# Fourier transform and two expert layers on one core: the first two rounds in written order, outputs of expert 1 kept in DRAM, weights of expert 2 made earlier, column sums by fp32r matmuls

## The chip, the cores and the metric

The kernel runs on one core of a Trainium2 chip. The metric is the time of one execution on the device in microseconds, less is better. The kernel before was timed three times.

## The reference

```python
X = np.fft.fft(np.fft.fft(x, axis=1), axis=2).real     # x: 2 x 3008 x 256
h = X.reshape(6016, 256) @ w_in                          # 256 x 2048
g = h * (1 / (1 + exp(-h)))                              # expert 1
x1 = g @ w_out                                           # 2048 x 256
h2 = x1 @ w_in2                                          # 256 x 2048, expert 2
g2 = max(h2, 0) + alpha * min(h2, 0)
out = g2 @ w_out2                                        # 2048 x 256
```

The weights of both experts come as float64 and are turned to float32 on the chip.

## The kernel before, in words

A float32 product is made of three fp32r products: each operand is split into a high part and a low part (the low part is the operand minus its high part), and high·high, high·low and low·high are summed. So nearly every tile has a `hi` made by ACT and a `lo` made by DVE or POOL.

**Start.** `stage_a` folds the input and makes the first Fourier stage, stores it in DRAM as `ys`, `load_y` (L302) reads it back transposed, `stage_b` (L311) makes the second stage: tiles `z`, six chunks of 502 columns, three for each of the two batches. `first_row` (L345) makes a row term `n` of a chunk by ones-matmuls. `prep_w1` (L389) turns a quarter of `w_in` to float32 (`to_f32`, four DVE steps), splits it, multiplies it by a small Fourier matrix on PE (`cw`, L424), takes a column sum `r` by fp32 matmuls (L428), and splits the result into `wi`. `prep_o1` does the like for `w_out`. The start is under `manual_schedule`: there every engine's queue holds its instructions in the order of the text.

**Rounds.** 96 rounds, one for each chunk and each 128 of the 2048 columns (`ORDER`). Round i: `eo_mm` (L554) makes `pe` and `po` (three matmuls each, L563 to L565); `mm2(i-2)` (L596) adds 12 matmuls of round i-2 into four accumulators `a` (L613 to L617, those of L615 read the low parts `gl`); `silu_split` (L568) makes `t`, `hp`, `t` on DVE (L571, L574, L575), four SiLU on ACT (L578, L579), and calls `low1(i-1)` (L585), which makes the two low parts `gl` of the round before (L591). The low part for s=1 is always on POOL; that for s=0 is on POOL where `lo_pool` says so (rounds up to 29 and 51 to 86), else on DVE. All other work is dealt out over the rounds by `PLAN` (L26): `put(a, b, steps)` (L862) spreads the steps of a key evenly over rounds a to b. In the rounds a planner sets the order on each engine from modelled times, and `leash` (L871) lets a round's dealt-out steps follow only after `t` of the round before and `gl` of the one before that. `i1` to `i3`, `o1` to `o3` are the quarters of expert 1's weights, `x`, `a`, `y`, `c` the second batch's transform, `w2` the conversion of expert 2's weights. A result of a chunk stays in SBUF as `O1[c]`, one of 12 large buffers (`big`) for each chunk.

**Expert 2.** Its first product uses Strassen's seven products on halves. `prep_ws` (L503) makes the sums and splits of the weights (`ws`, sums L523, lows L518), one set (`ws0`) and another (`ws1`); `prep_wo2` (L533) makes the split of the second weights (`wo`, ACT L542 and L165, lows on POOL L166); `split_o1` (L637) makes four differences (`xt`, L651) and five splits (`os`, L660 and POOL L661) of a half chunk. After the rounds, again in written order, 96 steps n follow: `outer(n)` (L684, products 1 and 5 into `ac`, copied by ACT to `e`, L691), `inner(n)` (L693, products 2, 6, 3), `seventh(n)` (L712), the prelu on ACT and DVE, and `mm4(n-2)` (12 matmuls, L773). Steps 0 and 1 hold the two last `mm2`. A plan key of 96 or more is a step: 97 is n = 1.

Of the kernel before, what the change touches and what calls it, by code (L numbers as in the profile page):

```python
# [32 lines left out]
}  # L33
W2_AHEAD = 2
# [4 lines left out]
    ["xs", "xs", "cs", "ch", "e128", "e128"] + [f"wi{g}_{j}" for g in (2, 3) for j in range(4)],  # L39
# [29 lines left out]
def _tables():  # L69
# [35 lines left out]
    c[:, OC0] = m % 2  # L105
# [15 lines left out]
def fft_moe_kernel(  # L121
# [267 lines left out]
    def prep_w1(g):  # L389
# [3 lines left out]
        def steps(h, v):  # L393
# [160 lines left out]
    def eo_mm(i):  # L554
# [3 lines left out]
        z = ZS[divmod(c, NCB)]  # L558
        pe, po = mm_ps(f"pe{i}", CW), mm_ps(f"po{i}", CW)
        for ps, j in ((pe, 0), (po, 2)):  # L560
            at = 128 * j + 128 * q
            hi, lo = (WI[1, g, 2 * h + k][:, at : at + 128] for k in range(2))
            nc.tensor.matmul(ps, hi, z[:, j, :], start=True, stop=False)  # L563
            nc.tensor.matmul(ps, lo, z[:, j, :], start=False, stop=False)  # L564
            LAST["pe", i] = nc.tensor.matmul(ps, hi, z[:, j + 1, :], start=False, stop=True)  # L565
        return pe, po

    def silu_split(i, pe, po):  # L568
# [221 lines left out]
    if True:  # L790
        with tc.manual_schedule():
# [23 lines left out]
            for h in range(2):  # L815
                load_y(0, h, 0)
# [86 lines left out]
        for pg in range(2):  # L903
            steps = prep_ws(pg)
            put(*PLAN[f"ws{pg}"], steps[:8])
            put(*PLAN[f"ws{pg}b"], steps[8:])
# [109 lines left out]
```

## Time and profile before

| | us |
|---|---|
| median of 3 runs | 974.41 |
| lowest, highest | 973.65, 975.18 |
| profiled execution | 972.72 |
| its span, first to last instruction | 970.9 |

| engine | busy us | share of the span |
|---|---|---|
| PE (matmuls) | 954.2 | 98% |
| DVE | 782.9 | 81% |
| ACT | 709.8 | 73% |
| POOL | 413.4 | 43% |

Busy time is the union of an engine's instructions. The mean granted TensorE clock over the span is 0.995 of full speed.

### The profile page before, as it was taken

The page shows a single profiled execution, that of the slowest core. Times are in us where ns is not written, and L with a number is a line of the kernel's source. Part 1 is how long each engine was busy: PE and PEld are TensorE (multiplying, and loading weights), DVE is VectorE, ACT ScalarE, POOL GpSimd, SP SyncE. Part 2 cuts the span into 40 slices and gives each one's busy share as a digit, 9 for nine tenths or more (in the row PEclk, how much of TensorE's full clock was granted, in tenths as well). Part 3 has the DMA queues.
Part 4 walks back from the last instruction along what each step waited for, and adds up shares of the span by engine and source line. Part 5 has one row for each costly group of instructions (what it writes and reads, how often), then busy time and mean ns, then how long its engine had stood idle before and what let it go on. Part 6 is the DMA issues. An engine that isn't in the chain of part 4 may idle for free.

```text
span 970.9 us, 14465 instructions
## 1 busy us (share of the span) xinstructions
PE 954.2 (98%) x5234; PEld 824.8 (85%) x5234; DVE 782.9 (81%) x1324; ACT 709.8 (73%) x1413; POOL 413.4 (43%) x356
## 2 busy tenths in 40 slices
PE   8999999999999999999999999999999999999997
PEld 6788887788888888887789999999999999999996
DVE  6778999787787888996688787887888888787875
ACT  3567667575576766777888887887878888887885
POOL 2468868763266767789522131221312212131200
PEclk9999999999999999999999999999999999999999
DMA  8921000006110120000000000000000000000000
GB/s 275 311 89 44 1 1 22 22 13 190 43 44 17 44 88 6 39 0 1 1 1 24 19 3 23 1 23 1 22 22 1 23 1 22 22 1 23 1 22 22
DMA packets 16039, 37.05 MB, mean 38 GB/s; under 512 B 1632, under 2 KB 11104, under 8 KB 13920
## 3 DMA queue, kind: packets, MB, share of 16 engines
q1 hardware_dynamic: 15968, 36.13, 11.2%
q8 instruction: 41, 0.67, 0.3%
q14 instruction: 30, 0.25, 0.1%
HBM read 26.81 MB, written 9.31 MB: 37 GB/s over the span
## 4 chain that ended last, share of the span: by engine, by line
PE 90%; DVE 4%; ACT 2%; POOL 2%; issue 1%; DMA 1%; SPq 0%; DVEq 0%
PE a L773 27%; PE ac L675 20%; PE a L615 8%; PE a L617 8%; PE a L613 8%; PE b L675 3%; PE pe L563 2%; PE pe L565 2%; PE pe L564 2%; PE po L563 2%; PE po L565 2%; PE po L564 2%; PE psb L321 1%; PE psa L277 1%; POOL gl L591 1%
## 5 line engine op out<-in xcount | busy, mean ns | idle before, releaser
L773 PE MATMUL a<-gh,wo 128*128 128x502 f32 x768 | 268.5, 391 | 0.0
L773 PEld LDWEIGHTS a<-gh,wo 128*128 128x128 f32 x768 | 145.1, 189 | 23.4
L742 DVE SCALAR_TENSOR_TENSOR h<-h,fc,q 128x502 f32<-128x502 f32 x192 | 129.9, 677 | 37.9 <-ACT q L737 35.1
L591 POOL TENSOR_TENSOR gl<-t,gh 128x502 fp32r<-128x502 f32 x96 | 132.7, 1383 | 52.5 <-ACT t L579 30.5
L615 PE MATMUL a<-gl,wo 128*128 128x502 f32 x384 | 147.5, 394 | 2.5 <-POOL gl L591 2.5
L773 PE MATMUL a<-gl,wo 128*128 128x502 f32 x384 | 149.6, 390 | 0.0
L617 PE MATMUL a<-gh,wo 128*128 128x502 f32 x384 | 146.3, 391 | 0.0
L578 ACT ACTIVATE gh<-hp 128x502 fp32r<-128x502 f32 x96 | 59.9, 624 | 114.9 <-DVE hp L574 114.1
L753 DVE TENSOR_TENSOR gl<-h,gh 128x502 fp32r<-128x502 f32 x192 | 140.7, 733 | 0.1
L748 ACT ACTIVATE gh<-h 128x502 fp32r<-128x502 f32 x192 | 118.4, 617 | 2.1 <-DVE h L742 2.1
L613 PE MATMUL a<-gh,wo 128*128 128x502 f32 x384 | 118.7, 395 | 0.5 <-DVE cvi L197 0.5
L737 ACT ACTIVATE q<-h,fc 128x502 f32<-128x502 f32 x192 | 116.9, 609 | 2.8 <-DVE h L720 1.5
L591 POOL TENSOR_TENSOR gl<-hp,gh 128x502 fp32r<-128x502 f32 x65 | 91.5, 1408 | 62.0 <-ACT hp L579 59.9
L651 POOL TENSOR_TENSOR xt<-o 128x252 f32<-128x252 f32 x24 | 16.7, 714 | 187.0 <-ACT q L737 168.3
L571 DVE SCALAR_TENSOR_TENSOR t<-n,sm,pe 128x502 f32<-128x502 f32 x96 | 70.2, 732 | 26.8 <-PE pe L565 22.9
L615 PEld LDWEIGHTS a<-gl,wo 128*128 128x128 f32 x384 | 72.7, 189 | 18.2 <-POOL gl L591 3.7
L613 PEld LDWEIGHTS a<-gh,wo 128*128 128x128 f32 x384 | 72.2, 191 | 16.4 <-ACT gh L578 1.5
L617 PEld LDWEIGHTS a<-gh,wo 128*128 128x128 f32 x384 | 72.7, 189 | 14.5
L773 PEld LDWEIGHTS a<-gl,wo 128*128 128x128 f32 x384 | 72.5, 189 | 7.6
L709 ACT ACTIVATE u<-ac 128x252 f32<-128x252 f32 x96 | 36.6, 381 | 54.6 <-PE ac L675 50.5
L574 DVE TENSOR_TENSOR hp<-t,po 128x502 f32<-128x502 f32 x96 | 64.5, 672 | 12.1 <-PE po L565 7.5
L661 POOL TENSOR_TENSOR os<-o,os 128x252 fp32r<-128x252 f32 x36 | 32.2, 907 | 92.8 <-ACT os L660 92.8
(177 smaller groups left out, 2292.7 us busy)
## 6 DMA issues: line engine op xcount, KB each, us to landing
out_t<-ot SPq DMA_DIRECT2D x24, 251.0 KB, 2.6
x<-in_xs SPq DMA_DIRECT2D x8, 512.0 KB, 5.2
raw_w<-in_wi SPq DMA_DIRECT2D x4, 1024.0 KB, 5.5
raw_w<-in_wo SPq DMA_DIRECT2D x4, 1024.0 KB, 4.8
raw_i<-in_wi SPq DMA_DIRECT2D x3, 1024.0 KB, 8.0
raw_o<-in_wo SPq DMA_DIRECT2D x3, 1024.0 KB, 5.7
y<-ys SPq DMA_DIRECT2D x16, 144.0 KB, 4.1
x<-in_xs SPq DMA_DIRECT2D x2, 1024.0 KB, 4.8
```

The costliest lines, as they stand in the source:

```text
L571: nc.vector.scalar_tensor_tensor(t, E128[c], odd_sb[:, f : f + 1], pe, op0=ALU.mult, op1=ALU.add)
L574: nc.vector.tensor_tensor(hp, t, po, op=ALU.add)
L591: LAST["gl", i] = (nc.gpsimd if s or lo_pool(i + 1) else nc.vector).tensor_tensor(lo, h, hi.bitcast(F32), op=ALU.subtract)
L613: nc.tensor.matmul(ACC1[lb, s], hi, G[i, s][0], start=st, stop=False)
L615: nc.tensor.matmul(ACC1[lb, s], hi, G[i, s][1], start=False, stop=False)
L617: nc.tensor.matmul(ACC1[lb, s], lo, G[i, s][0], start=False, stop=sp)
L675: nc.tensor.matmul(to, w, x, start=start and q == 0, stop=q == 2, skip_group_check=True)
L737: nc.scalar.activation(h["q", i][:, to], source(n, part), AF.Abs, scale=coef(n, i, 1))
L742: nc.vector.scalar_tensor_tensor(h[f"h{i}"][:, to], source(n, part), coef(n, i, 0), h["q", i][:, to], op0=ALU.mult, op1=ALU.add)
L748: nc.scalar.activation(hi, H[n][f"h{i}"], AF.Copy)
L753: nc.vector.tensor_tensor(lo, H[n][f"h{i}"], G[n, i][0].bitcast(F32), op=ALU.subtract)
L773: nc.tensor.matmul(ACC2[lb], w[lb][j], x, start=st and first, stop=sp and last)
```

## The change

`PLAN` is moved and gets new keys; the rest of the diff, cut to its core:

```diff
-    "o0": (0, 2), "c1": (1, 4), "c2": (4, 7), "i1": (5, 10), "o1": (9, 13),
-    "li2": (10, 11), "i2": (14, 20), "lo2": (13, 14), "o2": (19, 24), "li3": (18, 19), "i3": (23, 27), "lo3": (22, 23), "o3": (26, 29),
+    "o0": (2, 3), "c1": (1, 4), "c2": (4, 7), "i1": (4, 9), "o1": (8, 12),
+    "li2": (9, 10), "i2": (12, 18), "lo2": (12, 13), "o2": (17, 22), "li3": (16, 17), "i3": (21, 25), "lo3": (20, 21), "o3": (24, 28),
...
-    "y2": (65, 66), "c5": (67, 77), "w2": (50, 88),
-    "co": (60, 61), "ws0": (62, 80), "ws0b": (84, 92), "ws1": (80, 92), "ws1b": (93, 99),
-    "wo0": (86, 87), "wo1": (90, 91), "wo2": (97, 98), "wo3": (98, 100),
+    "y2": (65, 66), "c5": (67, 77), "w2": (50, 82),
+    "co": (60, 61), "ws0": (62, 80), "ws0b": (84, 92), "ws1": (82, 92), "o1r": (80, 81), "os": (85, 93),
+    "wo0": (87, 90), "wo1": (91, 94), "wo2": (98, 100), "wo3": (100, 102),
+O1_AHEAD = 14
-    ["xs", "xs", "cs", "ch", "e128", "e128"] + [f"wi{g}_{j}" for g in (2, 3) for j in range(4)],
+    ["xs", "xs", "cs", "ch", "e128", "e128"] + [f"big{j}" for j in range(8)],
...
-                r = mm_ps(f"r{g}_{h}", 2)
+                r = mm_ps(f"r{g}_{h}", 4)
                 for q in range(2):
-                    w = t[0][:, 128 * q : 128 * q + 128]
-                    nc.tensor.matmul(r[:, q : q + 1], w, cs[:, OC0 : OC0 + 1], start=True, stop=True)
+                    for j in range(2):
+                        w = e[j][:, 128 * q : 128 * q + 128]
+                        nc.tensor.matmul(r[:, 2 * q : 2 * q + 2], w, co, start=j == 0, stop=j == 1)
...
-                nc.scalar.activation(w, w, AF.Copy, scale=fc[:, 2, f : f + 1])
-            hi, lo = (WO[2, g, j].rearrange("p f e -> p (f e)")[:, h * 512 : h * 512 + 512] for j in range(2))
-            split(hi, lo, v, nc.gpsimd)
+                v = V2["o", g // 2][:, o + 256 * q : o + 256 * q + 256]
+                hi, lo = (WO[2, g, j][:, 2 * h + q, :] for j in range(2))
+                sign = fc[:, 2, f : f + 1]
+                nc.scalar.activation(hi, v, AF.Copy, scale=sign)
+                nc.vector.scalar_tensor_tensor(lo, v, sign, hi.bitcast(F32), op0=ALU.mult, op1=ALU.subtract)
...
-        return i < LO_POOL or 52 <= i < 88
+        return 2 < i < LO_POOL or 52 <= i < 88
-            LAST["gl", i] = (nc.gpsimd if s or lo_pool(i + 1) else nc.vector).tensor_tensor(
+            LAST["gl", i] = (nc.gpsimd if (s and i < NC * NF - 2) or lo_pool(i + 1) else nc.vector).tensor_tensor(
...
+            if f == NF - 1:
+                store_o1(c)
+    def store_o1(c):
+        OD[c] = dp.tile([128, 4 * CW], F32, name=f"od{c}")
+        nc.sync.dma_start(OD[c], O1[c].rearrange("p k n -> p (k n)"))
+    def load_o1r(c):
+        O1[c] = big([128, 4, CW], F32, f"o1r_{c}")
+        nc.sync.dma_start(O1[c].rearrange("p k n -> p (k n)"), OD[c])
...
-            for h in range(2):
-                load_y(0, h, 0)
+            load_y(0, 0, 0)
...
             nc.scalar.activation(ch, cc, AF.Copy)
+            nc.gpsimd.tensor_copy(co, cs[:, OC0 : OC0 + 2])
+            load_y(0, 1, 0, nc.scalar)
...
-            run(s0[:3])
+            run(s0)
             warm(cs[:, FA0 : FA0 + 128], cs[:, :256], WARM[1])
             b00, b01 = stage_b(0, 0), stage_b(0, 1)
             run(b00[:2])
+            run(p0)
             run(b01[:2])
-            run(post1[4:5])
-            first_row(0, 0)
-            run(post1[5:])
-            run(s0[3:])
-            run(p0)
+            ps0 = eo_mm(0, lambda: first_row(0, 0))
+            ps1 = eo_mm(1)
             run(s1[:EARLY_O0])
+            silu_split(0, *ps0, lambda: run(post1[4:]))
+            silu_split(1, *ps1)
...
-        put(n1 - 5, n1 - 1, split_o1(0))
-        for i in range(n1):
+        put(*PLAN["o1r"], [lambda: load_o1r(0)])
+        put(*PLAN["os"], split_o1(0))
+        for i in range(2, n1 - 1):
...
         with tc.manual_schedule():
-            low1(n1 - 1)
+            pe, po = eo_mm(n1 - 1)
+            outer(0)
+            mm2(n1 - 1 - LAG)
+            silu_split(n1 - 1, pe, po)
+            run(plan.pop(n1 - 1, []))
             for n in range(NP + 2):
...
+                c = (n + O1_AHEAD) // 16
+                if (n + O1_AHEAD) % 16 == 0 and c < NC:
+                    load_o1r(c)
...
-                if new:
+                if 0 < n < NP:
                     outer(n)
...
+                if n == 0:
+                    low1(n1 - 1)
```

Each chunk's result goes to DRAM when it is finished and is read back 14 steps before its block of 16 steps (chunk 0's in round 80). The buffers that this frees take the second half of `ws1`, so `ws1` no longer waits for `wi` of the last rounds. The function of `eo_mm` is split in two halves so that something can be called between them, and `silu_split` gets the same; between `hp`, `t` and the SiLU of round 0 stand now the Fourier product, the column sum and the split of the first quarter's second half (`post1[4:]`).

## Rows read from the trace of the kernel before

**Rows 1.** Windows: us, busy of PE, PEld, DVE, ACT, POOL (instructions), granted clock, DMA share, GB/s.

```profile
20.00:40.00 20.00, 17.74 (x98) 15.13 (x99) 15.81 (x29) 9.66 (x24) 4.38 (x3) 0.91 0.98 296
...
140.00:160.00 20.00, 18.92 (x92) 15.26 (x91) 18.14 (x24) 12.50 (x24) 15.12 (x13) 1.00 0.00 1
160.00:180.00 20.00, 18.66 (x81) 14.30 (x79) 14.97 (x19) 12.20 (x22) 19.30 (x15) 1.00 0.08 26
...
400.00:420.00 20.00, 20.00 (x89) 16.53 (x88) 18.28 (x26) 15.20 (x29) 16.34 (x13) 1.00 0.00 1
420.00:440.00 20.00, 20.00 (x89) 16.38 (x88) 17.48 (x21) 15.24 (x29) 16.84 (x13) 1.00 0.01 1
440.00:460.00 20.00, 17.91 (x79) 14.38 (x78) 14.91 (x20) 15.47 (x29) 20.00 (x18) 0.98 0.00 0
460.00:480.00 20.00, 17.85 (x101) 15.32 (x101) 11.24 (x22) 15.89 (x35) 8.15 (x8) 0.94 0.01 1
```

**Rows 2.** Timeline of PE after round 95: start, us, instruction [idle before <-releaser].

```profile
459.12 0.78 PE L615 MATMUL a<-gl,wo 128*128 128x502 f32 x1 [1.69 <-POOL gl L591]
...
468.78 0.50 PE L675 MATMUL ac<-os,ws_6h 128*128 128x252 f32 x2 [1.64 <-ACT e L691]
...
471.37 0.50 PE L675 MATMUL ac<-os,ws_7h 128*128 128x252 f32 x2 [0.27 <-DVE h L710]
```

**Rows 3.** Timeline of POOL in the same stretch.

```profile
454.47 2.95 POOL L661 TENSOR_TENSOR os<-xt,os 128x504 fp32r<-128x504 f32 x2
457.38 2.90 POOL L591 TENSOR_TENSOR gl<-t,gh 128x502 fp32r<-128x502 f32 x2
...
461.47 1.27 POOL L518 TENSOR_TENSOR ws_6l<-v2w,ws_6h 128x512 fp32r<-128x512 f32 x1
```

**Rows 4.** Groups of POOL and DVE: busy us, mean ns of one | idle before.

```profile
L591 POOL TENSOR_TENSOR gl<-t,gh 128x502 fp32r<-128x502 f32 x96 | 132.7, 1383 | 52.5 <-ACT t L579 30.5 <-DVE gl L591 7.6 <-PE pe L565 6.8
L661 POOL TENSOR_TENSOR os<-xt,os 128x504 fp32r<-128x504 f32 x24 | 38.2, 1610 | 50.0 <-ACT os L660 50.0
L661 POOL TENSOR_TENSOR os<-o,os 128x252 fp32r<-128x252 f32 x36 | 32.2, 907 | 92.8 <-ACT os L660 92.8
L651 POOL TENSOR_TENSOR xt<-o,xt 128x252 f32<-128x252 f32 x24 | 22.6, 941 | 0.9
L166 POOL TENSOR_TENSOR wo<-v2o,wo 128x512 fp32r<-128x512 f32 x8 | 11.1, 1400 | 13.7 <-ACT wo L165 13.7
L518 POOL TENSOR_TENSOR ws_5l<-v2w,ws_5h 128x512 fp32r<-128x512 f32 x2 | 3.0, 1520 | 0.0
...
L591 DVE TENSOR_TENSOR gl<-hp,gh 128x502 fp32r<-128x502 f32 x31 | 30.0, 967 | 5.0 <-ACT hp L579 4.6
```

**Rows 5.** Timeline of POOL in round 86 and of PE that uses its results.

```profile
419.08 1.74 POOL L518 TENSOR_TENSOR ws_7l<-v2w,ws_7h 128x512 fp32r<-128x512 f32 x1
420.79 3.44 POOL L166 TENSOR_TENSOR wo<-v2o,wo 128x512 fp32r<-128x512 f32 x2
424.19 1.27 POOL L591 TENSOR_TENSOR gl<-hp,gh 128x502 fp32r<-128x502 f32 x1
...
426.07 0.39 PE L615 MATMUL a<-gl,wo 128*128 128x502 f32 x1
```

**Rows 6.** Timeline of the start: SP's and ACT's queues, and PE in rounds 0 and 1.

```profile
19.56 1.71 SPq L308 DMA_DIRECT2D y<-ys  x4
...
19.93 0.63 ACT L407 ACTIVATE wi<-we 128x512 fp32r<-128x512 f32 x1 [2.33 <-DVE we L404]
...
33.51 0.91 PE L321 MATMUL psb<-cs,y 96*128 96x94 f32 x6 [0.30 <-DVE t L571]
35.41 1.17 PE L321 MATMUL psb<-cs,y 96*128 96x94 f32 x6 [0.99 <-DVE t L575]
...
35.19 0.61 ACT L578 ACTIVATE gh<-hp 128x502 fp32r<-128x502 f32 x1
```

**Rows 7.** The column sums' matmuls: count, duration ns min/median/max.

```profile
L428 PE MATMUL r<-cs,we x32: 165/250/250, 22.3 to 155.3; 128*128 128x1 f32 x32
```

More of the change, by code (lines that the diff above doesn't have):

```diff
@@ L104, in _tables @@
     c[0, SG0 : SG0 + 128] = 1
-    c[:, OC0] = m % 2
+    c[:, OC0 : OC0 + 2] = (m % 2)[:, None]
     c[0, OD0 : OD0 + 128] = m % 2
@@ L228, in fft_moe_kernel @@
     cl = wp.tile([128, SG0 - CD0], F32R, name="cl")
+    co = wp.tile([128, 2], F32R, name="co")
     X = {}
@@ L300, in stage_a, with load_y @@
         return fold, mm, rest
-    def load_y(b, h, kh):
+    def load_y(b, h, kh, queue=None):
         w = (K_PARTS[kh + 1] - K_PARTS[kh]) // 2
@@ L307, in load_y @@
         for j in range(2):
-            last = nc.sync.dma_start(Y[b, kh][48 * j : 48 * j + 48, h, :w, :], src[j])
+            last = (queue or nc.sync).dma_start(Y[b, kh][48 * j : 48 * j + 48, h, :w, :], src[j])
         return last
@@ L424, in fold @@
                         nc.tensor.matmul(to, w, x, start=j == 0, stop=j == len(run_) - 1)
-                r = mm_ps(f"r{g}_{h}", 2)
+                r = mm_ps(f"r{g}_{h}", 4)
                 for q in range(2):
-                    w = t[0][:, 128 * q : 128 * q + 128]
-                    nc.tensor.matmul(r[:, q : q + 1], w, cs[:, OC0 : OC0 + 1], start=True, stop=True)
+                    for j in range(2):
+                        w = e[j][:, 128 * q : 128 * q + 128]
+                        nc.tensor.matmul(r[:, 2 * q : 2 * q + 2], w, co, start=j == 0, stop=j == 1)
                 f = 4 * g + 2 * h
-                nc.scalar.activation(odd_sb[:, f : f + 2], r, AF.Copy)
+                nc.scalar.activation(odd_sb[:, f : f + 2], r[:, ::2], AF.Copy)
             def fold_high():
@@ L490, in coefficients @@
         eng.tensor_tensor(two, two, fc[:, 2, :], op=ALU.mult)
+    QUARTERS = {}
     def slab(home, name):
+        if home[:3] == "big":
+            j, q = divmod(int(home[3:]), 4)
+            if j not in QUARTERS:
+                QUARTERS[j] = big([128, 4, 512], F32R, f"wsb_{j}")
+            return QUARTERS[j][:, q, :]
         if home in ("cs", "ch"):
@@ L552, in fft_moe_kernel, with eo_half @@
     MORE = [False]
-    def eo_mm(i):
+    def eo_half(i, ps, j):
         c, f = ORDER[i]
@@ L558, in eo_mm, with silu_split @@
         z = ZS[divmod(c, NCB)]
-        pe, po = mm_ps(f"pe{i}", CW), mm_ps(f"po{i}", CW)
[L560 to L565, printed above, removed]
+        at = 128 * j + 128 * q
+        hi, lo = (WI[1, g, 2 * h + k][:, at : at + 128] for k in range(2))
+        nc.tensor.matmul(ps, hi, z[:, j, :], start=True, stop=False)
+        nc.tensor.matmul(ps, lo, z[:, j, :], start=False, stop=False)
+        LAST["pe", i] = nc.tensor.matmul(ps, hi, z[:, j + 1, :], start=False, stop=True)
+    def eo_mm(i, between=None):
+        pe, po = mm_ps(f"pe{i}", CW), mm_ps(f"po{i}", CW)
+        eo_half(i, pe, 0)
+        if between:
+            between()
+        eo_half(i, po, 2)
         return pe, po
-    def silu_split(i, pe, po):
+    def silu_split(i, pe, po, between=None):
         c, f = ORDER[i]
@@ L575, in silu_split @@
         LAST["t", i] = nc.vector.tensor_tensor(t, t, po, op=ALU.subtract)
+        if between:
+            between()
         for s, h in ((0, hp), (1, t)):
@@ L628, in mm2 @@
             del G[i, 0], G[i, 1]
+            if f == NF - 1:
+                store_o1(c)
+    OD = {}
+    def store_o1(c):
[4 more added lines that the diff above has]
+        nc.sync.dma_start(O1[c].rearrange("p k n -> p (k n)"), OD[c])
     OS = {}
@@ L902, in fft_moe_kernel @@
         put(*PLAN["co"], [coefficients])
[L903 to L906, printed above, removed]
+        steps = prep_ws(0)
+        put(*PLAN["ws0"], steps[:8])
+        put(*PLAN["ws0b"], steps[8:])
+        put(*PLAN["ws1"], prep_ws(1))
         for g in range(4):
             put(*PLAN[f"wo{g}"], prep_wo2(g))
-        put(n1 - 5, n1 - 1, split_o1(0))
-        for i in range(n1):
+        put(*PLAN["o1r"], [lambda: load_o1r(0)])
+        put(*PLAN["os"], split_o1(0))
+        for i in range(2, n1 - 1):
             pe, po = eo_mm(i)
-            if i >= LAG:
-                mm2(i - LAG)
+            mm2(i - LAG)
             silu_split(i, pe, po)
-            leash(i, plan.pop(i, []))
+            leash(i, plan.pop(0, []) + plan.pop(1, []) + plan.pop(i, []))
         with tc.manual_schedule():
-            low1(n1 - 1)
+            pe, po = eo_mm(n1 - 1)
[3 more added lines that the diff above has]
+            run(plan.pop(n1 - 1, []))
             for n in range(NP + 2):
```

2 lines of the change are left out of this document (removed).

## The prediction

> **What bounds the kernel now.** I read the page first: PE is busy for 954.2 of 970.9 us, no other engine above 81%, and the chain that ended last is PE for 90% of the span. So time can only come from PE's gaps, from its clock, or from matmuls that go away; the change takes none away. The windows in stretches of 20 us then tell where the gaps are [rows 1]. The reader is to see that PE is busy for all 20.00 us of most stretches, while DVE stands at 91% and ACT at 76% beside it, and that four stretches differ: 20 to 40 (start, 2.26 us idle), 140 to 160 and 160 to 180 (1.08 and 1.34), and 440 to 480 (2.09 + 2.15 = 4.24), which is the passage from the rounds to the steps of expert 2. The clock falls in the first and in the last: a mean grant of 0.91 over 20 us is 2 x 0.09 x 20 = 3.6 us at 1.2 instead of 2.4 GHz, which costs 1.8; 0.98 and 0.94 are 0.8 + 2.4 = 3.2 us at the lower level, which cost 1.6. Start 4.1, middle 2.4, passage 5.8: some 12 us are all that there is to gain.
>
> Next the timeline of PE in the passage says who was late [rows 2]: POOL's `gl` (1.69 us), ACT's `e` (1.64), DVE's `h11`/`h12` (0.27); smaller pieces are left. The timeline of POOL says why [rows 3]: `gl` of rounds 94 and 95 queues behind two large `os` lows, and POOL still makes `ws` lows at 461. A round takes 18 matmuls; 89 in 20 us [rows 1] are 0.225 us each, 4.05 us a round.
>
> All sums are against the profiled execution, 972.72 us (span 970.9 and 1.8 around it); the median of the runs is 1.69 higher.
>
> **The passage: -3.7.** Both lows of rounds 94 and 95 go to DVE, `os` and `ws1` are dealt out to round 93, so the waits for POOL and the clock that falls behind them should go. `wo2` moves from step 1, where ACT made both its parts ahead of `e`, to steps 2 and 3, `wo3` to 4 and 5. What is late next: `seventh(0)` needs `h12` on DVE, and before `h11` and `h12` DVE now has four lows of 0.97 [rows 4], between them `hp` and `t` of round 95 and the wait for four SiLU of 0.61 [rows 6]. That is 3.9 + 2 x 0.97 at most for `hp` and `t` + about one SiLU, 6.4, and then `h11` and `h12`. PE has until then mm2(93), mm2(94) (24 x 0.225 = 5.4) and 15 matmuls of half the width (1.7): 7.1 us. They come out about even; I take 0.7, between 0 and the 1.64 of the wait for `e`. In steps 2 to 5 each part of `wo` costs ACT two short copies and DVE two short lows, at the time when ACT also makes `os` of the next half chunk: 0.35 a step, 1.4, an estimate near the 0.27 row; bounds 0 and twice 1.64. Left 2.1 of 5.8: -3.7, from -5.8 to -0.9.
>
> **POOL in rounds 84 to 92: +2.0.** This is the price of making it early. By the plan POOL has there 13 `gl` (13 x 1.383 = 18.0), five lows and three sums of `ws1` and three lows of `ws0` (11, all taken at 1.52: 16.7); four differences `xt` (3.8) and five `os` (3 x 0.907 + 2 x 1.61 = 5.9) [rows 4]. Together 44.4 us in 9 x 4.05 = 36.4: 8 over. The same count for before (13 `gl`, 5 of `ws`, four `wo` of 1.40, four `xt`, one `os`) gives 36, yet the windows show 16.34 and 16.84 of 20 busy, 83%, or 30.2 [rows 1], since the planner runs dealt-out work later than its rounds. By the measured share the new load is 30.2 + 8.4 = 38.6, 2.2 over. There is no cover: in round 86 two `wo` and a `ws` low delayed `gl` until its matmul began 0.6 us after it [rows 5]. Rounds 93 to 95 have room (3 x 2.7 us). I take 2.0, between 0 and 8.0. The conversion `w2`, on DVE and ACT, ends six rounds earlier and so is denser by a fifth in rounds 50 to 82; the stretch 400 to 420 had conversions, `gl` and `ws` with DVE at 91% and no gap on PE [rows 1], so 0; if DVE falls behind, it is in the range of rival C. `wo` on DVE adds eight pairs of short lows in rounds 87 to 94 where the conversions have ended: 0.
>
> **Start: -0.4.** SP issues four `y` loads in 1.71 us [rows 6], 0.43 each. Two of them move to ACT's queue, behind `ch` and ahead of `wi` high (L407). SP could issue at 19.56 only when the stores of `ys` had landed; ACT waits for the stores of the other half too, then issues for 0.85 us, so `wi` high starts at about 20.4 instead of 19.93 and DVE's low and PE's first `cw` go 0.5 later. Against that: rounds 0 and 1 no longer stand behind the second half of the quarter's product on DVE, `t` and `hp` come earlier, and PE's waits for `t` (0.30 and 0.99 [rows 6]) shrink; but the SiLU of round 0, at 35.19 before, now stand behind that product's copy on ACT and so gain little. `gl` of rounds 0 and 1 for s=0 go to a free DVE. Of 4.1 I let 0.9 go and pay 0.5. Bounds -3 and +2 (the ACT queue's wait in full, no gap closed). The DMA engines gain nothing of it that I count. The page "DMA: Bandwidth & Descriptors" of the Trainium skill (section "Issuing engines are not separate DMA queues") says that issuing from a second engine saves only issue time; by it the second half could land 0.85 us earlier, and the sum would be the same, as PE's warming matmuls stand ahead of the reader.
>
> **Middle: -0.9.** `i2`, `o2`, `i3`, `o3` run over rounds 12 to 28 instead of 14 to 29, two rounds ahead of their use, with less overlap. Of 2.4 us idle in 140 to 180 I let the first 0.9 go; the folds of the second batch, which cause most of the rest, keep their rounds. The planner writes a new order, so the bounds are -2.4 and +2.4.
>
> **At nothing.** Column sums: 32 matmul records of one column at 0.25 us before [rows 7], 32 matmuls of two columns after; 0, with a quarter of 8.0 us on either side as bound. Stores and loads of `O1`: 12 transfers on SP with DMA at most 0.16 busy after 140 us in the windows shown [rows 1], reloads asked for 14 steps ahead; 0. In SP's queue a store waits for its accumulators' copies, and behind it wait loads that are dealt out two rounds (8 us) ahead; above 0 only if that is used up. An 0.85 us bound each for six stores is 5.
>
> **Sum.** -3.7 + 2.0 - 0.4 - 0.9 = -3.0: 969.7 for the profiled execution, 971.4 for the median.
>
> **Rivals.**
> A, nothing is paid back: the planner spreads POOL's work into rounds 93 to 95. For it: these rounds have 8 us of room. Against it: the queue of round 86 [rows 5]. Passage -5.3, start -1.0, middle -1.6: -7.9, 966.5.
>
> B, gaps move instead of going: the ACT queue's wait is paid in full and rounds 0 and 1 only trade waits (+1.5), the middle's gaps change place (0). For it: DVE is the bound at the start (15.81 of 20 while PE waits), and its work stays. Passage -3.7, POOL +2.0: -0.2, 974.2.
>
> C, slower: POOL bounds rounds 84 to 92, because the leash puts dealt-out steps ahead of the next `gl`, as in round 86 [rows 5]. All 8.0 us over are paid by PE; `os` comes late, so the clock falls again (1.6 of the passage's gain). -3.7 + 1.6 + 8.0 - 1.3 = +4.6: 979.0. It turns the sign when POOL is over by more than 3.7 + 0.4 + 0.9 = 5.0 us. For it: 8 over by the plan, and the lows now on DVE may hold POOL up: `gl` on DVE takes 0.97 in the rounds [rows 4]. Against it: measured 83%. The Trainium skill, "SBUF — State Buffer", section "SBUF: two separate sides", states that DVE with two SBUF inputs and POOL exclude each other for a whole instruction; by that rule the 16 lows of `wo` moved to DVE and the five of `gl` there still take POOL's time, which makes this rival likelier than its own row says; no row here shows a lock as such.
>
> **How the numbers follow.** Forecast 0.50 (own range 968.5 to 974.0), A 0.17, B 0.18, C 0.15. A measurement of this kernel can tell 0.2%, 1.9 us, from no change: faster is below 972.5, slower above 976.4. Of the forecast 0.70 is faster, 0.28 the same; all of A is faster; B 0.20, 0.60, 0.20; C is slower but for 0.04. Faster 0.35 + 0.17 + 0.04 = 0.56, same 0.14 + 0.11 = 0.25, slower 0.19. The range of 8 in 10 cuts the outer part of A and of C: 965.5 to 978.5.
>
> **What would show it.** Passage: the windows after the rounds with some 2 us idle and the grant at 1.00, no wait of PE for POOL there, one for DVE's `h12` in step 0. Rounds 84 to 92: waits of PE for `gl` on POOL, 2 us in all; 0 is A, 6 or more is C. Start: `wi` high later than 20, its window's idle and grant little changed. Middle: idle between 1 and 2 us. The forecast is wrong if the passage still loses 4 us or more, if rounds 84 to 92 lose more than 5, or if the start moves by more than 3.

## The result, and the profile after

The changed kernel takes 983.19 us in the median of 4 runs (981.85 to 985.64), the kernel before 974.79 beside it (4 runs, 973.65 to 976.09): ratio 1.0089, 95% interval 1.0065 to 1.0112. It is slower by 8.4 us, where 971.4 was forecast. The profiled execution of after took 983.16 us, its span is 981.4, 10.5 longer than that of before.

The windows of after answer to those of before [rows 1]; the columns are the same.

```profile
20.00:40.00 20.00, 16.76 (x87) 13.62 (x87) 13.88 (x28) 8.71 (x20) 1.28 (x1) 0.91 0.92 288
120.00:140.00 20.00, 19.27 (x85) 15.63 (x83) 19.00 (x26) 12.38 (x22) 15.82 (x12) 1.00 0.00 1
140.00:160.00 20.00, 15.77 (x66) 12.35 (x67) 17.84 (x23) 9.58 (x18) 14.62 (x12) 0.91 0.00 0
160.00:180.00 20.00, 20.00 (x94) 16.74 (x94) 16.52 (x23) 13.63 (x25) 15.88 (x12) 1.00 0.09 27
400.00:420.00 20.00, 19.20 (x84) 15.28 (x83) 16.28 (x23) 14.12 (x25) 15.43 (x13) 1.00 0.13 52
420.00:440.00 20.00, 19.20 (x84) 15.37 (x83) 16.75 (x23) 15.15 (x29) 19.50 (x18) 1.00 0.01 1
440.00:460.00 20.00, 19.04 (x82) 14.91 (x81) 19.51 (x24) 14.55 (x29) 19.86 (x15) 1.00 0.00 1
460.00:480.00 20.00, 20.00 (x112) 17.45 (x111) 15.15 (x28) 15.73 (x31) 2.54 (x2) 1.00 0.04 16
480.00:500.00 20.00, 17.93 (x109) 14.87 (x108) 16.91 (x33) 14.20 (x34) 5.67 (x7) 1.00 0.24 88
```

The reader is to see three things. The passage now runs without a gap: 460 to 480 has PE busy for 20.00 us at a clock of 1.00, where before had 17.85 at 0.94. In the middle PE is idle for 4.2 us of one window, at a clock of 0.91. And the passage is now framed by loss: 0.8 to 1.0 us in each window from 400 to 460, with POOL at 19.5 and 19.9 of 20, and 2.07 us in 480 to 500.

A window that starts at a fixed time holds other work in each kernel. So I put marks on the work: the start of the first matmul of `mm2(r)` that reads `gl`, for round r, and of the first of `mm4(s)` that reads `gl`, for step s. The difference of a stage's length between a kernel and the profiled run of before, in us (`mm2(r)` runs in round r+2 and `mm4(s)` in step s+2, so the stages are named by the work, not by the round in which it runs):

```
           to r4  r4-22 r22-32 r32-68 r68-84 r84-93 r93-s0  s0-s5 s5-end  whole
after       +1.2   +2.5   +3.7   -0.1   +2.6   +3.5   -7.3   +4.4   -0.1  +10.4
a_early      0.0   -0.5   +0.6   +0.2   +4.9   +1.9   -7.3   +4.4   -0.6   +3.8
a_start     +0.9    0.0   +2.5   +0.1   +3.4   +3.4   -7.3   +4.4   +0.5   +7.9
a_wo        +1.9   +2.5   +3.8   -0.1   +3.6   +3.9   -7.3   +1.8   +0.2  +10.4
a_w2        +1.3   +2.5   +3.7   -0.1   -0.1   +5.9   -7.3   +4.4   -0.2  +10.0
b_early     +1.3   -1.5   +2.1   -0.1    0.0   +0.2   -1.7   -0.1   -0.5   -0.3
b_pass      +0.8    0.0    0.0    0.0    0.0   +5.0   -7.3   +1.9   -0.7   -0.3
a_nowo      +0.3   -0.5   +0.6   +0.2   +3.3   +1.8   -7.3   -1.1   -0.6   -3.3
b_w95       +2.2    0.0    0.0    0.0    0.0   +6.4   -3.3    0.0   -1.1   +4.2
a_nosums    +2.2   +2.8   +1.8   +0.4   +3.3   +3.6   -7.3   +4.4   -0.9  +10.3
a_late3     +4.6   +2.4   -1.4   +0.5   +3.2   +3.6   -7.3   +4.4   -0.5   +9.7
b_best1     +2.7    0.0    0.0    0.0   +0.5   +3.2   -6.9   +0.6   -0.8   -0.6
b_best1r    +1.2    0.0    0.0    0.0   +0.6   +3.2   -6.9   +0.6   -0.7   -1.9
b_best3     +1.5    0.0    0.0    0.0   +1.0   +1.6   -5.8   +0.6   -0.6   -1.6
```

Read the first line: the passage gave 7.3 us, rounds 68 to 93 took 6.1 and steps 0 to 5 another 4.4, so that the three together lose 3.2. Rounds 4 to 32 lost 6.2 more. The first column is scatter: the kernels that have before's start lie between 0.0 and +2.7 there (8 traces, mean 1.3), those with the written start between 0.0 and +4.6 (7 traces, mean 1.6). The times scatter too: the kernel before took 971.53 to 977.20 us in 19 runs of one session, with a mean granted clock of 0.998 in the fastest and 0.993 in the slowest. So below stages are compared, and a single time proves little.

Two things have to be taken off before a column is read as a loss. The first is work that a new order puts on the other side of a mark. These are PE's matmuls of `pe` and `po` between marks 4 and 22, first in before, then in after:

```profile
59.90:141.50 81.60, 30.71 (x113) 1.00 0.11 38
61.10:145.10 84.00, 28.85 (x104) 1.00 0.10 34
```

After has nine fewer there and nine more behind mark 22; at 0.225 us each that is 2.0 us. So after loses 4.5 in rounds 4 to 22 and 1.7 in 22 to 32, and the same 2.0 changes columns in every kernel with group 3's keys early (a_start, a_wo, a_w2, b_early, a_nosums). At mark 93 six matmuls of half the width, 0.7 us, change sides wherever round 95 is written out (after loses 2.8 in 84 to 93 and gains 6.6 in the passage), and at mark 84 it is 0.7 to 1.1 us in the b_best kernels. Sums over 4 to 32 or over 68 to step 0 are free of this.

The second is the clock. A stretch at 1.2 GHz costs 1.7 us (worked out for b_pass below), and after the same waits it can come or stay away. a_early and a_nowo, which have the same code there, both wait 0.92 and then 0.58 or 0.57 us for DVE's `t` between 401 and 404; these are their next 4 us, a_early first:

```profile
404.00:408.00 4.00, 4.00 (x13) 3.20 (x11) 3.70 (x6) 3.94 (x9) 3.37 (x3) 0.58 0.51 211
404.00:408.00 4.00, 4.00 (x19) 3.36 (x18) 3.70 (x7) 3.97 (x8) 3.13 (x3) 1.00 0.46 191
```

Between round 4 and step 5 such a stretch lies in the passage of before (b_early has the same waits of 1.69 and 1.64 us there, no stretch, and is 1.7 shorter), in 22 to 32 of after, a_wo, a_w2 and b_early, in 4 to 22 of a_nosums, in 68 to 84 of a_early and in 84 to 93 of a_w2 and b_pass; b_w95 has one twice as long around mark 93, and the other traces have none.

The middle. First PE's waits in after, 60 to 200 us (what it waited for: us in total, times, longest), then the timeline (start, us, instruction, idle before and its releaser) of DVE, POOL, ACT and PE around the largest.

```profile
PE cw L426 <- ACT wi L409: 2.0, 1, 2.0
PE a L630 <- DVE o L639: 1.9, 2, 1.4
PE po L571 <- DVE wi L440: 1.5, 1, 1.5
```

```profile
137.32 1.32 DVE L186 TENSOR_SCALAR cvi<-cvi 128x512 f32<-128x512 f32 x1
138.56 1.50 DVE L190 TENSOR_SCALAR cvi<-cvi 128x512 uint32<-128x512 uint32 x1
...
143.88 1.77 DVE L198 SCALAR_TENSOR_TENSOR cvi<-raw_i,cvi 128x512 uint32<-128x512 uint32 x1
...
137.08 1.27 POOL L608 TENSOR_TENSOR gl<-hp,gh 128x502 fp32r<-128x502 f32 x1 [0.35 <-ACT hp L596]
138.31 1.47 POOL L608 TENSOR_TENSOR gl<-t,gh 128x502 fp32r<-128x502 f32 x1
143.35 1.74 POOL L608 TENSOR_TENSOR gl<-hp,gh 128x502 fp32r<-128x502 f32 x1 [3.57 <-ACT hp L596]
145.72 0.74 POOL L403 TENSOR_TENSOR we<-cvi 128x256 f32<-128x256 f32 x1 [0.64 <-DVE cvi L198]
146.42 1.17 POOL L406 TENSOR_TENSOR we<-cvi 128x256 f32<-128x256 f32 x1
...
147.62 0.63 ACT L409 ACTIVATE wi<-we 128x512 fp32r<-128x512 f32 x1 [2.89 <-POOL we L406]
...
145.93 0.39 PE L634 MATMUL a<-gh,wo 128*128 128x502 f32 x1
148.31 0.39 PE L426 MATMUL cw<-wi,ch 128*128 128x256 f32 x1 [1.99 <-ACT wi L409]
...
150.02 0.62 PE L572 MATMUL po<-z,wi 128*128 128x502 f32 x1
150.44 0.62 PE L573 MATMUL po<-z,wi 128*128 128x502 f32 x1
```

Follow it backwards. PE stands at `cw` of a late quarter of the weights, which waits for ACT's `wi`, that for POOL's `we`, that for the last conversion step `cvi` on DVE, and this took 1.77 us. After the wait the matmuls follow each other by 0.42 us, where 0.225 is usual [rows 1]: the granted clock is 0.62 in 148 to 152, so the wait is paid nearly twice. In a_start the same wait is followed by a clock of 1.00 and paid once. The windows and the wait, after first:

```profile
148.00:152.00 4.00, 3.69 (x11) 3.04 (x12) 1.94 (x4) 4.00 (x9) 4.00 (x5) 0.62 0.00 0
...
145.55 0.38 PE L426 MATMUL cw<-wi,ch 128*128 128x256 f32 x1 [1.98 <-ACT wi L409]
145.00:149.00 4.00, 3.45 (x16) 2.88 (x17) 2.68 (x5) 4.00 (x8) 4.00 (x5) 1.00 0.00 0
```

Around the passage, after has these waits of PE between 340 and 520 us:

```profile
PE ac L704 <- DVE h L739: 1.9, 5, 0.7
PE po L571 <- DVE t L590: 1.5, 3, 0.7
PE a L802 <- DVE gl L782: 1.4, 3, 0.7
PE pe L571 <- DVE t L586: 1.0, 2, 0.8
PE po L571 <- DVE t L586: 0.7, 2, 0.6
```

All of them are for DVE, none for POOL. Two pieces of DVE's timeline show why, one of round 87 and one of step 3:

```profile
431.30 1.12 DVE L554 SCALAR_TENSOR_TENSOR wo<-v2o,fc,wo 128x256 fp32r<-128x256 f32 x1 [1.56 <-ACT wo L553]
432.35 0.67 DVE L589 TENSOR_TENSOR hp<-t,po 128x502 f32<-128x502 f32 x1
432.94 1.62 DVE L554 SCALAR_TENSOR_TENSOR wo<-v2o,fc,wo 128x256 fp32r<-128x256 f32 x1
434.48 0.67 DVE L590 TENSOR_TENSOR t<-t,po 128x502 f32<-128x502 f32 x1
...
485.53 0.88 DVE L554 SCALAR_TENSOR_TENSOR wo<-v2o,fc,wo 128x256 fp32r<-128x256 f32 x2 [0.84 <-ACT wo L553]
486.33 0.74 DVE L771 SCALAR_TENSOR_TENSOR h<-h,fc,q 128x502 f32<-128x502 f32 x1
```

The lows of `wo` stand at the head of DVE's queue and wait there for ACT, with `hp`, `t` and the prelu behind them, and half of such a low takes 1.1 to 1.6 us in the rounds, but 0.88 for two in the steps, where POOL is nearly idle.

### The profile page after: what moved, and what is told of

Same layout as the page of the kernel before. It is cut to its first block, busy times and chain, and to the rows that moved or that the text cites. A ratio compares the mean times of both kernels' runs of the same rounds, so it can differ in the third digit from the quotient of the medians.

```text
span 981.4 us, 14501 instructions
## 1 busy us (share of the span) xinstructions
PE 958.6 (98%) x5234; PEld 824.0 (84%) x5234; DVE 801.0 (82%) x1344; ACT 705.1 (72%) x1405; POOL 397.5 (41%) x345
## 4 chain that ended last, share of the span: by engine, by line
PE 74%; DVE 14%; ACT 6%; issue 4%; DMA 1%; POOL 1%; ACTq 0%; DVEq 0%; SPq 0%; POOLq 0%
PE a L802 25%; PE ac L704 19%; PE a L630 5%; PE a L632 5%; PE a L634 5%; PE b L704 3%; DVE hp L589 2%; DVE t L586 2%; ACT gh L595 2%; PE po L571 1%; PE pe L571 1%; PE po L573 1%; PE po L572 1%; PE pe L573 1%; DVE t L590 1%
## 5 line engine op out<-in xcount | busy, mean ns | idle before, releaser
L608 POOL TENSOR_TENSOR gl<-t,gh 128x502 fp32r<-128x502 f32 x94 | 129.9, 1382 | 67.5 <-ACT t L596 47.5
L608 POOL TENSOR_TENSOR gl<-hp,gh 128x502 fp32r<-128x502 f32 x63 | 87.5, 1389 | 69.3 <-ACT hp L596 54.1
L680 POOL TENSOR_TENSOR xt<-o1r 128x252 f32<-128x252 f32 x24 | 16.9, 726 | 204.1 <-ACT q L766 113.3
L704 PE MATMUL ac<-os,wsb 128*128 128x252 f32 x576 | 90.6, 279 | 1.3 <-DVE h L739 1.3
L704 PEld LDWEIGHTS ac<-os,wsb 128*128 128x128 f32 x576 | 80.5, 188 | 6.3 <-DVE h L739 2.8
```

The source lines that it names most:

```text
L608: LAST["gl", i] = (nc.gpsimd if (s and i < NC * NF - 2) or lo_pool(i + 1) else nc.vector).tensor_tensor(lo, h, hi.bitcast(F32), op=ALU.sub ...
L704: nc.tensor.matmul(to, w, x, start=start and q == 0, stop=q == 2, skip_group_check=True)
```

## Experiments

Kernels called a_ are the changed kernel with one part undone, those called b_ the kernel before with one part done. Times of before are those of the same session.

**First session: undo one part (before 973.52).**

a_early, the early keys back at before's rounds:

```diff
-"i1": (4, 9), "o1": (8, 12), ... "i2": (12, 18), ... "o2": (17, 22), ... "i3": (21, 25), ... "o3": (24, 28),
+"i1": (5, 10), "o1": (9, 13), ... "i2": (14, 20), ... "o2": (19, 24), ... "i3": (23, 27), ... "o3": (26, 29),
```

> The changed kernel with the keys of expert 1's weights (i1 to o3 and their loads) put back to their rounds of before, all else as changed. Theory (the moved keys cost the middle): the middle, 100 to 165 us, loses 6 us more than before in the changed kernel; here that falls to 1 or less, the total is about 977.5. Rival (the written order of rounds 0 and 1 leaves DVE behind, and the middle pays for it): the middle keeps its 6 us, total 983. Second rival (any edit gives the planner another order, and stalls move about): the middle loses something between 2 and 8, at other places.

976.51 us. Rounds 4 to 32 lose 0.2 instead of 6.2; passage and steps stay, and rounds 68 to 93 lose 6.8 instead of 6.1, 1.7 of it the clock stretch at 404. Without the moved keys there is no loss in the middle, so neither rival holds.

a_start, before's start in the changed kernel (rounds 0 and 1 left to the planner, `y` loads on SP, the first lows on POOL):

> The changed kernel with the start as before: rounds 0 and 1 planned, the y loads all on SP, the first lows on POOL again; all else as changed. Theory (the start costs its own 1.5 us and nothing later): the first mm2 comes 1.5 us earlier, the middle keeps its loss, total about 981.5. Rival (the start is what puts the middle behind): round 32 comes 6 us or more earlier, total about 976.

980.64. The start's own share is within its scatter. Rounds 4 to 32 still lose 2.5 instead of 6.2, with the same three large waits as after (2.0, 1.9 and 1.8 us in all); 1.7 of the difference is the clock stretch that does not come here. So the written start takes part in the loss with some 2 us, between the theory (0) and the rival (6).

a_wo, the lows of `wo` on POOL again:

```diff
...
-                nc.scalar.activation(hi, v, AF.Copy, scale=sign)
-                nc.vector.scalar_tensor_tensor(lo, v, sign, hi.bitcast(F32), op0=ALU.mult, op1=ALU.subtract)
...
+                nc.scalar.activation(w, w, AF.Copy, scale=fc[:, 2, f : f + 1])
...
+            split(hi, lo, v, nc.gpsimd)
```

> The changed kernel with the low parts of expert 2's second weights on POOL and in three operations, as before. Theory (DVE waits at the head of its queue for ACT's copy, and PE then for DVE): the waits of PE for h12 and for gl in steps 2 to 5 (3.3 us) go, and some 2 of the 5 us lost in rounds 68 to 93; total 977 to 979. Rival, as the prediction had it (POOL bounds these rounds): POOL gets 8 x 1.4 = 11 us more in rounds 87 to 94 and PE waits longer for gl there: total 985 or more.

983.28, both theories wrong in part. Steps 0 to 5 fall from 4.4 to 1.8, rounds 68 to 93 rise from 6.1 to 7.5, and there PE now waits for POOL:

```profile
PE a L632 <- POOL gl L608: 2.4, 2, 1.6
```

The wait moves with the work.

a_w2, `w2` at its old pace:

```diff
-"w2": (50, 82),
+"w2": (50, 88),
```

> The changed kernel with the conversion of expert 2's weights dealt to rounds 50 to 88 instead of 50 to 82. Theory (the denser conversion makes DVE's t late in rounds 70 to 82): the waits of PE for t between 360 and 415 us (2.5 us) go, rounds 84 to 88 get a little of it back; total 981 to 982. Rival (those waits come from another order or from O1's transfers): they stay, total 983.

982.74. Rounds 68 to 84 lose nothing instead of 2.6, so the denser `w2` was not free, as the theory had it. Rounds 84 to 93 lose 2.4 more, but 1.7 of that is a clock stretch that after does not have there; the time is above the theory's 981 to 982.

**Second session: do one part (before 976.29).**

b_early, the early keys alone:

> The kernel before with only the moved keys of the first rounds (i1 to o3 and their li/lo keys one to two rounds earlier; o0 and the start as before). Theory (the earlier keys by themselves put the conversions beside PE's folds where VectorE can't make both): the stretch from round 4 to round 32 loses 3 to 5 us against before, round 32 stands at +3 to +5, and the time is 977 +-1.5. Rival (the keys only hurt together with the written start, whose rounds 0 and 1 run further ahead of the conversions): round 32 within +-1 of before, the time 973.5 +-1.

972.71, and round 32 at +1.9, of which 1.3 is the start: the rival, 0.6 for rounds 4 to 32. The parts -1.5 and +2.1 are the work that crosses mark 22; without it they are 0.5 and 0.1. PE's largest wait in the middle is another than in after, 1.99 us for ACT's `gh` at 144, in place of the 2.4 us that before is idle in 140 to 180. So the early keys alone cost next to nothing; they cost only beside the rest of the change.

b_pass, the passage alone:

```diff
...
-"ws1": (80, 92), "ws1b": (93, 99), "wo0": (86, 87), "wo1": (90, 91), "wo2": (97, 98), "wo3": (98, 100),
+"ws1": (82, 92), "o1r": (80, 81), "os": (85, 93), "wo0": (87, 90), "wo1": (91, 94), "wo2": (98, 100), "wo3": (100, 102),
```

and with it the slabs in freed rows, `O1` by way of DRAM and round 95 written out.

> The kernel before with the passage alone changed: expert 1's outputs through DRAM, the slabs of page 1 in their freed rows, round 95 written out with outer(0) in it, the last lows on VectorE, wo2 and wo3 two rounds later; start, early keys, column sums, w2's pace and the lows of wo on POOL as before. Theory (the passage only gives what rounds 80 to 94 and steps 2 to 5 pay): round 32 at 0 +-0.5, round 93 at +4 to +7, step 0 0 to +1, steps 2 to 5 +2 to +3, the time 975 to 977. Rival (what after loses in rounds 68 to 94 comes from the denser w2 and from wo on VectorE, and the passage by itself keeps its gain): round 93 at +2 or less, the time 967 to 970.

972.49. The stages are the theory's (+5.0, -7.3, +1.9), and their sum is -0.4 where a gain of 5 was the rival; the time is under its 975 to 977, since the passage gave 1 to 2 us more than it had put there (step 0 stands at -1.4, not between 0 and +1). Here is where rounds 84 to 93 pay it, in POOL's and PE's timeline and in the windows:

```profile
424.82 1.30 POOL L526 TENSOR_TENSOR ws_7l<-v2w,ws_7h 128x512 fp32r<-128x512 f32 x1
426.08 1.74 POOL L526 TENSOR_TENSOR wsb<-v2w,wsb 128x512 fp32r<-128x512 f32 x1
427.76 1.08 POOL L678 TENSOR_TENSOR xt<-o1r,xt 128x252 f32<-128x252 f32 x1
428.80 1.25 POOL L606 TENSOR_TENSOR gl<-hp,gh 128x502 fp32r<-128x502 f32 x1
...
427.93 0.39 PE L571 MATMUL pe<-z,wi 128*128 128x502 f32 x1
430.11 0.79 PE L630 MATMUL a<-gl,wo 128*128 128x502 f32 x1 [1.80 <-POOL gl L606]
430.69 0.62 PE L632 MATMUL a<-gh,wo 128*128 128x502 f32 x1
```

```profile
426.00:430.00 4.00, 1.94 (x8) 0.98 (x6) 3.71 (x5) 4.00 (x9) 4.00 (x4) 1.00 0.00 0
430.00:434.00 4.00, 3.89 (x11) 3.18 (x12) 2.62 (x4) 3.16 (x8) 4.00 (x4) 0.57 0.00 0
```

`gl` stands behind two splits and a difference, PE waits 1.80 us, and the clock granted in the next 4 us is 0.57, which is 1.2 GHz for most of them: 2 x 0.43 x 4 = 3.4 us at the lower level, which cost 1.7 more. Here a wait of 1.8 us was paid twice.

a_nowo, a_early with the lows of `wo` left out:

> The changed kernel with before's early keys, as in a_early (976.5), and besides the low halves of expert 2's wo left out: the product takes the high half in their place, so the number of TensorE's instructions stays and 16 VectorE operations of 1.1 to 1.6 us go. Theory (rounds 84 to 94 and steps 2 to 5 are short of VectorE and POOL time): round 93 falls from +7.2 to +3 or less, steps 2 to 5 cost at most 1 instead of 4.4, the time is 969 to 972. Rival (the order of the steps there, ScalarE's halves ahead of the silus, is what is late): steps 2 to 5 still cost over 3, the time is 975 or more.

969.42. Steps 0 to 5 go from +4.4 in a_early to -1.1, as the theory said; rounds 68 to 93 only from 6.8 to 5.1, as it did not (round 93 stands at +5.7, not +3). And that 1.7 lies in 68 to 84, ahead of the first low of `wo`: it is the clock stretch of a_early at 404. In 84 to 93, where the lows are, it is 1.9 and 1.8. So the lows of `wo` on DVE cost 5.5 us in the steps and about 0.1 in the rounds; the loss there belongs to `os`, `ws1` and the denser `w2`.

b_w95, round 95 alone:

```diff
-        for i in range(n1):
+        for i in range(n1 - 1):
...
+            pe, po = eo_mm(n1 - 1)
+            outer(0)
+            mm2(n1 - 1 - LAG)
+            silu_split(n1 - 1, pe, po)
```

> The kernel before with only round 95 written out (outer(0) between its matmuls, the lows of rounds 94 and 95 on VectorE); nothing else of the change. Theory (the passage's loss before, some 7 us, was POOL's and VectorE's leftover of ws and wo work, not the order of round 95): the time is 972 to 974, the loss between round 93 and step 2 falls by 2 at most. Rival (the order of the lows and of outer(0) is what held the passage): that loss falls by 4 or more, the time is 968 to 970.

976.91. From round 84 to step 0 it loses 3.1, 6.4 ahead of mark 93 against 3.3 gained behind it, so neither forecast came. PE's waits there:

```profile
PE ac L675 <- POOL os L661: 4.8, 1, 4.8
PE ac L675 <- ACT e L691: 1.6, 1, 1.6
```

`outer(0)` now stands ahead of `mm2(93)` and waits for the `os` that POOL still has to make. So what held before's passage was unfinished work, not the order, and the new order only makes sense with `os` made early.

**Third session (before 972.06).**

a_nosums, the column sums as before:

> The changed kernel with the column sums as before (fp32 on the column of constants, from t, instead of fp32r from the two halves e). In the changed kernel rounds 4 to 32 lose 6.2 us; the early keys alone on the kernel before lost 0.6 there, and the changed kernel without them lost 0.2. Theory (the keys with the written start: two of the three parts suffice): rounds 4 to 32 still lose 5 to 7 us, the time is 982 to 984. Rival (the keys with the sums, which wait for both halves e and so stand later in PE's queue): they lose 2 or less, the time is 976.5 to 979.5.

983.07, near the theory: rounds 4 to 32 still lose 4.6 (its range was 5 to 7), so the sums are not what the early keys collide with. Whether the other 1.6 is theirs, one trace doesn't tell. PE's large waits are others than in after, 1.8 us for ACT's `o` at 102 and 1.8 for DVE's `gl` at 181, so the chain at `cw` belongs to one order of the planner and not to the early keys as such.

b_best1, the work of b_pass laid elsewhere:

```diff
-"o1r": (80, 81), "os": (85, 93), ... "wo2": (98, 100), "wo3": (100, 102),
+"o1r": (68, 69), "os": (70, 84), ... "wo2": (97, 101), "wo3": (101, 105),
```

> The passage alone (b_pass, 972.5 beside 976.3 of before) with expert 1's outputs read back and split in rounds 68 to 84 instead of 80 to 93, where GpSimd had 2 to 9 us free of 20, and the four steps of wo2 and wo3 spread over rounds 97, 99, 101 and 103. Theory (b_pass paid 4.7 us in round 86, where a low on GpSimd came behind the splits, and some 2 in steps 2 to 5 for the steps of wo; both are a matter of where the work lies): rounds 84 to 93 lose 1 or less instead of 5.0, steps 2 to 5 lose 1 or less instead of 2.2, the time is 966 to 968.5. Rival (the work is conserved: the same microseconds turn up in rounds 70 to 84 or in steps 0 to 8): the sum of both stays over 5 us and the time is 972 or more.

972.10, no gain by this single time; by stages rounds 68 to 93 lose 3.7 and steps 0 to 5 lose 0.6, together 4.3 instead of 6.9; 1.7 of the 2.6 is the clock stretch of b_pass. Neither all bad placing nor all conserved.

**Fourth session (before 974.42, 19 runs).**

a_late3, group 3's keys alone put back:

```diff
-"li3": (16, 17), "i3": (21, 25), "lo3": (20, 21), "o3": (24, 28),
+"li3": (18, 19), "i3": (23, 27), "lo3": (22, 23), "o3": (26, 29),
```

> The changed kernel with the keys of group 3 alone (li3, i3, lo3, o3) put back to before's rounds; i1, o1, li2, i2, lo2, o2 stay one to two rounds earlier. In the changed kernel rounds 4 to 22 lose some 2.5 us in small waits and 23 to 32 another 3.7. Theory (each earlier key makes conversions lie beside PE's folds with no VectorE time left, so the loss is spread over all of them): round 32 at +3 to +5, the time 979 to 981. Rival (only group 3, whose conversions meet the fold of group 2 at round 23 to 25, costs): round 32 at +2 or less, the time 976 to 978.5.

982.40, with a start 4.6 late (a mean grant of 0.91 over its first 60 us, where after has 0.97). Counted from round 4, rounds 4 to 32 lose 1.1, which is the rival's size. With group 3's keys put back 5.1 of the middle's 6.2 go, 1.7 of them the clock stretch; 1.1 is left with the keys of groups 1 and 2.

b_best1r:

> The kernel of b_best1 again, timed in three rounds: from round 4 on it was 3.3 us shorter than the profiled run of before, but round 4 itself came 2.7 later in it, in code that is the same (the kernels with before's start had round 4 anywhere from 0 to +2.7). Theory (that difference is the start's own scatter): over the rounds it is faster, ratio 0.996 to 0.999. Rival (the later start belongs to it): ratio 1.000 +-0.001.

972.60 (10 runs), ratio 0.9988 [0.9972, 1.0004]: its middle is the theory's, its interval reaches the rival. In the second trace round 4 stands at +1.2 instead of +2.7, and the stages after it repeat within 0.1: the start scatters, the rest does not.

b_best3, the crowded rounds thinned out:

```diff
-"ws0b": (84, 92), "ws1": (82, 92), ... "wo0": (87, 90), "wo1": (91, 94),
+"ws0b": (84, 94), "ws1": (84, 97), ... "wo0": (88, 92), "wo1": (93, 97),
```

> b_best1 with page 1's splits dealt out over rounds 84 to 96 instead of 82 to 91, the last of page 0's to round 93 and wo0 and wo1 one to two rounds later: GpSimd was busy 19.2 of 20 us in rounds 85 to 89 and 2.6 of 20 from round 95 on. Theory (the 2.9 us that b_best1 still waits in rounds 85 to 88 are VectorE operations stretched beside GpSimd's, so thinning that work out takes them away): rounds 84 to 93 lose 1 or less, the passage after them no more than 1 of it back, ratio to before 0.993 to 0.997. Rival (the work comes up again as a wait for a slab in steps 0 to 4): ratio 0.998 to 1.001.

972.40 (10 runs), ratio 0.9973 [0.9960, 0.9987]: faster than before, just past the weak end of the theory. Against b_best1r it is not faster by the traces: rounds 84 to 93 fall from 3.2 to 1.6, but the passage gains 1.1 less (-5.8 instead of -6.9) and rounds 68 to 84 lose 0.4 more, so that rounds 68 to step 0 stand at -3.2 in one and -3.1 in the other; the medians differ by 0.2. The windows show what is left:

```profile
400.00:420.00 20.00, 20.00 (x89) 16.55 (x88) 18.38 (x23) 14.60 (x27) 17.54 (x13) 1.00 0.13 52
420.00:440.00 20.00, 18.58 (x81) 14.52 (x80) 18.68 (x25) 13.40 (x26) 15.11 (x11) 1.00 0.00 0
```

In 420 to 440 POOL is down from 19.2 of 20 in b_best1 to 15.1, but DVE is at 18.7, and PE waits for its `t`.

## Why the prediction was wrong

The forecast was -3.0 against the profiled execution of before, the profiled execution of after gives +10.4. By the terms of the sum, in us:

| term | forecast | measured | |
|---|---|---|---|
| start | -0.4 | +1.2 | the code with before's start scatters from 0.0 to +2.7 |
| middle | -0.9 | +6.2 | outside its bounds of 2.4; 1.7 is a clock stretch |
| `w2` denser, rounds 68 to 84 | 0 | +2.6 | |
| rounds 84 to 93 | +2.0 | +3.5 | inside 0 to 8; 0.7 is work that crosses mark 93 |
| passage with steps 0 to 5 | -3.7 | -2.9 | -7.3 and +4.4 |
| the rest | 0 | -0.2 | |

**The failed step is the middle**: "ahead of their use, with less overlap. Of 2.4 us idle in 140 to 180 I let the first 0.9 go". It had the wrong sign by far more than scatter, and is 7.1 of the 13.4 us between forecast and result. I took an earlier key as relief, because the consumer comes later. But a key says only when steps may be issued, and the steps then stand in four engines' queues, among the rounds' own work. In after `cw` of group 3 stands in PE's order ahead of rounds' matmuls, at the end of the chain of four engines in the timeline, and PE waits 1.99 us for it. a_early shows that without the earlier keys nothing is lost (0.2), a_late3 that 5.1 of the 6.2 go with group 3's keys alone. But the keys are not enough: alone on the kernel before they lose 0.6 (b_early), with before's start in the changed kernel 2.5 (a_start). What in the written start and in the rest of the change makes them costly is not settled; no run took that apart, and a_nosums loses 4.6 by other waits. Nor does DVE's busy share tell: it is 19.0 and 17.8 of 20 us from 120 to 160 in after, beside a POOL at 15.8 and 14.6, but before has 18.9 and 18.1 there, beside 12.8 and 15.1, with only 1.1 us of idle PE [rows 1 and this window of before]:

```profile
120.00:140.00 20.00, 20.00 (x95) 16.77 (x94) 18.93 (x29) 13.03 (x24) 12.79 (x11) 1.00 0.00 1
```

The range of the term was wrong in kind: for a key whose steps go through four engines, a wait on PE and the clock behind it can come anywhere, and 2.4, the idle that was there before, bounds only the gain. None of the three signs that the prediction named for being wrong came true; the middle was not among them.

**`w2` denser and `wo` on DVE "at nothing".** I read a stretch with DVE at 91% and no gap on PE as cover. a_w2 shows 2.6 us for the fifth more of conversions (3.2 to 3.6 in the other kernels that have it, without the clock stretch of a_early): at 91% there was none. For `wo` the rounds were right (a_nowo: about 0.1), the steps wrong: 1.4 was forecast for steps 2 to 5, 4.4 came, and a_nowo puts 5.5 on the lows there. I added up short operations; what they cost is the place at the head of DVE's queue while ACT is late (0.84 us in step 3).

**The passage.** The mechanism was right: no wait for POOL, a clock of 1.00. The size was off on both sides. The passage itself gave 7.3 instead of 5.1; 0.7 of that is work that crosses mark 93, and the 0.7 for "what is late next" did not come. 1.7 of it is the clock stretch that before's trace has there and b_early's, with the same waits, has not: against b_early the passage gives 5.6.

**POOL in rounds 84 to 92.** 2.0 forecast, 3.5 measured. That it lies inside the bounds is luck: the mechanism was POOL's late `gl`, and PE waits there for DVE's `t` and never for POOL. Rival C took this for the bound; its price (8.0) did not come; the kernel is slower all the same, by other terms. What I missed is how DVE and POOL share. In the trace of after a conversion (L198) takes 683 ns in the median where no POOL instruction overlaps it (674 to 692, 12 of them) and 1442 where one does (up to 1773, 20 of them); L190, with one tensor as input, 419 and 1169; the lows of `wo` (L554) 484 and 1220. `hp` and `t`, which read PSUM, take 665 and 677, 677 and 678: nothing. In the timeline above the two conversions at 137.32 and 138.56 end 0.3 us after the POOL instruction that was running when they began. The Trainium skill, "SBUF — State Buffer", section "SBUF: two separate sides", says this as a rule: DVE in its fast two-port modes, or with two SBUF inputs beside a POOL instruction that reads SBUF, and POOL take a shared pair of ports for a whole instruction each. These durations agree with it. The prediction quoted the rule and then left it out of the sum, because its busy shares were taken as free time. They are not: a DVE at 91% beside a POOL at 82% [rows 1] holds waiting for each other. In before one conversion step of expert 2's weights takes 419 ns at least and 1375 in the median (count, duration ns min/median/max):

```profile
L189 DVE TENSOR_SCALAR v2o<-v2o x8: 419/1375/1497, 304.7 to 415.3; 128x512 uint32<-128x512 uint32 x8
```

How much of the middle's loss this sharing makes is argued, not shown: no run took POOL's work out of those rounds.

**Why b_best3 gains so little.** Before's passage lost PE 4.24 us and, in this trace, the clock behind it because some POOL and DVE work was left over. Making it early moves it to rounds where DVE and POOL stand at 18 and 16 of 20. It still pays 1.0 + 1.6 + 0.6 for 5.8, and b_best1r, with other places, pays 0.6 + 3.2 + 0.6 for 6.9: nearly the same sum.

## What to carry to other kernels

Before moving work ahead to fill a wait later, add up in the stretch it goes to what the engines that share a port do together; a busy share of 90% was no room here. A step that goes through several engines costs by the queue in which it stands first and waits, not by its own length, and an earlier key can put it there. Compare kernels by marks on the work itself: single times of this one scatter by 5.7 us, while stages of unchanged code and order between rounds 4 and 84 repeat within 0.1 where the clock does the same. Then count the matmuls between the marks and look at the clock: here 2.0 us of work that crossed a mark, and 1.7 us of a clock stretch, each looked like the cost of a key.

## What the runs showed of the hardware

A DVE instruction on SBUF operands took up to 2.6 times its time beside POOL (683 to 1773 ns), with one tensor as input even 3.6 times (419 to 1506), while one with a PSUM input kept its time within 2%. A wait of PE of 1.8 to 2.0 us was followed by 4 us at a mean granted clock of 0.57 or 0.62 in b_pass (at 430) and after (at 148), but by 1.00 in a_start after 1.98 us (at 145); after waits of 0.92 and 0.58 us a_early had 0.58, a_nowo after 0.92 and 0.57 had 1.00. So the length of a wait does not by itself tell whether the clock falls. The start, the same code in 8 kernels, ended up to 2.7 us apart from trace to trace.
